# One ring of three PSUM slots, seven results turned into x by a transposing DMA, and new orders for the later stages of a sparse-attention + FFN kernel

## The chip, the core and the metric

The kernel runs on one core of one Trainium2 chip. A core has a matrix engine (TensorE, PE in the profile, with PEld for its weight loads), a vector engine (VectorE, DVE), a scalar engine (ScalarE, ACT), GpSimd (POOL) and a sync engine (SyncE, SP) that here only issues DMAs. Each engine works through its own list of instructions in order and waits on semaphores. The metric is the device time of one launch in microseconds (us), as the median over runs.

## The reference

```python
scores = 1/sqrt(64) * q @ k^T             # 4 batches, 8 heads, 768 tokens, head size 64
mask   = |block_i - block_j| <= 1, or block 0 / 23 on either side, or one of 3 sampled blocks   # 24 blocks of 32
attn   = softmax(where(mask, scores, -1e9))
x      = (attn @ v), heads side by side    # 3072 tokens x 512
out    = gelu(x @ w_in) @ w_out            # 512 -> 2048 -> 512, exact gelu, float32 out
```

Blocks 0 and 23 of each batch see all 24 blocks (the dense ones); each of the other 22 sees eight blocks: first, last, its three neighbours and three sampled ones.

## The kernel before

The work is cut into eight units, two per batch, of 384 tokens each. An even unit holds the blocks 1 to 11 and both dense blocks of its batch, an odd one the blocks 12 to 22. The attention of unit n+1 runs beside the second matrix product (FFN2) of unit n; between two such stages stands the first product (FFN1) of the unit whose attention has just ended, alone on PE. So the kernel alternates: attention n+1 with FFN2 n, then FFN1 n+1, and so on, and a last FFN2 alone.

In an attention stage a unit is cut into rounds (two sparse blocks of 32 queries, or one dense block for half of the heads) and groups (a, b, c: up to four sparse blocks; d: the dense ones). The order on every engine is written by hand: `attention` walks through a string of words, `PLANS[n]`. The number behind a letter is a round, the letter behind it a group.

- s: scores of a round on PE into a PSUM tile `sc` (line 358). m: row maxima on DVE (384, dense 387). e: exponentials on ACT (401, dense 405). t: 32x32 turnings on DVE (418, 423).
- w: values on PE into a PSUM tile `av` (445 dense, 484). d: division by the row sums on DVE (499 to 504), which writes `xh`.
- o: `xh` is turned by four PE transposes into a PSUM tile `tx` (516) and copied by ACT into `xT` (524, 529), the input of FFN1. O: the same in two copies.
- f: some of the 48 FFN2 products (583). S: store of finished FFN2 tiles, if there are any (ACT copy 567, then a DMA on SP). G: the gelu table is loaded on ACT (429).

An FFN1 step (540) puts two products of 384 columns into a PSUM tile `hp`; ACT makes the gelu of it (562; 560 for the last step). FFN1 needs the whole `xT`, since each product runs over all 384 columns.

PSUM has eight banks. Tiles `sc`, most `hp` and a few `av` take turns in two slots of two banks each (`psA`); most `av` and one or two `hp` have a slot of their own (`psV`); `psT` and `psO` (one bank each) hold the FFN2 tile and, in the other one, `tx`. A tile can be written only when the reader of the tile that had its slot before is done.

During an FFN1 stage DVE copies keys and values that the next unit will see into a buffer `gb` (`gather_fixed`, lines 296 and 309, and `gather`, 317). After FFN1 of units 1 and 3, POOL also issues twelve loads of later queries and keys (127); a small copy `mark` on POOL (173) holds them back until `xT` of the unit's second but last group (group b) has been written. POOL's own copies into `gb` wait behind these loads. SP turns the loaded queries and keys by transposing DMAs (137, 134).

Of the kernel before, what the change touches and what calls it, by code (L numbers as in the profile page):

```python
# [10 lines left out]
F32 = mybir.dt.float32  # L11
# [9 lines left out]
def kernel(  # L21
# [42 lines left out]
    psA = ctx.enter_context(tc.tile_pool(name="psA", bufs=2, space=PSUM))  # L64
    psV = ctx.enter_context(tc.tile_pool(name="psV", bufs=1, space=PSUM))
# [201 lines left out]
    def spaces():  # L267

        def banks():
            return [psT.tile([P, PI, PP], BF16, name="pt", tag="T"),  # L270
                    psO.tile([P, PI, PP], BF16, name="pt", tag="op")]
        views = [psA.tile([P, 2, 1024], BF16, name="pk", tag="A")[:, 0, 0:S].rearrange(
            "p (i c) -> p i c", i=PI) for _ in range(2)]
        yield from views + banks()
        two = psV.tile([P, 2, 1024], BF16, name="pq", tag="V")
        two = [two[:, i, 0:S].rearrange("p (i c) -> p i c", i=PI) for i in range(2)]
        yield from two[0:1] + banks() + two[1:2]
# [61 lines left out]
    closing = [unit for unit in units if unit.dense or unit.b == B - 1]  # L339
# [91 lines left out]
    def values(unit, grp, halves, ends_last=False):  # L431
        kv = kvs[unit.b % 2]
        if 0 in halves:

            pool, tag = (psA, "A") if unit in closing and grp == unit.ends[len(unit.rounds) - 1] else (psV, "V")
            st[grp, "av"] = pool.tile([P, 2, 512], F32, name="av", tag=tag)
# [57 lines left out]
    def divided(grp):  # L494
        av, n, m = st.pop((grp, "av"))
        rows = slice(0, 32 * n)
        a = av[rows, :, 0:VS * m // 2].rearrange("p h (g v) -> p h g v", v=VS)
        den = small.tile([P, 2, 4], F32, name="den")
        nc.vector.tensor_scalar_add(den[rows, :, 0:m].rearrange("p h (g x) -> p h g x", x=2),
                                    a[:, :, :, 2 * D:V2], 1e-9)  # L500
        rec = small.tile([P, 2, 4], F32, name="rec")
        nc.vector.reciprocal(rec[rows, :, 0:m], den[rows, :, 0:m])
        xh = small.tile([P, 2, 4 * D], BF16, name="xh")
        nc.vector.tensor_tensor(  # L504
            xh[rows, :, 0:m * D].rearrange("p h (g x d) -> p h g x d", x=2, d=D),
            a[:, :, :, 0:2 * D].rearrange("p h g (x d) -> p h g x d", d=D),
            rec[rows, :, 0:m].rearrange("p h (g x) -> p h g x", x=2)[:, :, :, :, None].to_broadcast([32 * n, 2, m // 2, 2, D]),
            op=ALU.mult)
        st[grp, "xh"] = xh, n, m

    def outputs(unit, grp, parts=1):
        xh, n, m = st.pop((grp, "xh"))
        T = turning_bank([P, 2, 2, P], "tx")
        for h in range(2):
            for G in range(m // 2):
                nc.tensor.transpose(T[:, G, h, 0:32 * n],  # L516
                                    xh[0:32 * n, h, P * G:P * G + P],
                                    identity[0:32 * n, 0:32 * n])
# [12 lines left out]

    opened, covered = {}, {}

    def ffn1_tile(n, m):
        pool, tag = (psV, "V") if m == (4 if n else 2) else (psA, "A")
        return pool.tile([P, 2, 512], F32, name="hp", tag=tag)
# [14 lines left out]
    def ffn1_step(n, m):  # L551
        T = P * len(units[n].quads)
        hp = opened.pop(m) if m in opened else ffn1_tile(n, m)
        last = psV.tile([P, 2, 512], F32, name="hp", tag="V") if m == KOUT - 2 else None
# [45 lines left out]
    def last_output(n):  # L600
# [5 lines left out]
                 psV.tile([P, 2, D_MODEL], F32, name="av", tag="V")[:, 0],  # L606
# [9 lines left out]
    def attention(unit, filler, plan, extra={}, ahead=None):  # L616
# [12 lines left out]
        for word in plan.split():  # L629
# [32 lines left out]
            elif what in "oO":  # L662
                outputs(unit, groups[arg], 1 + (what == "O"))
            todo.remove(word.lower())
# [79 lines left out]
    def next_keys(b):  # L744
# [108 lines left out]
```

## Time and profile before

| | |
|---|---|
| median of 3 runs | 274.27 us (274.2 to 274.39) |
| span of the profiled execution, first to last instruction | 271.9 us |
| time of the profiled execution beside its span | not given apart; the median of the runs is 2.4 us above the span |
| PE / ACT / DVE / POOL busy | 255.1 / 207.0 / 203.2 / 103.0 us |
| FFN1 stages (each, from 72.2 us on) | 10.4 us, PE busy throughout |
| attention stages of units 2 to 7 | 20.3, 18.0, 20.0, 17.9, 19.8, 17.0 us |

A stage is read in the table of windows: the share of an engine's busy time in it says which engine could bound it, and the chain of waits which one did. PE is busy 94% of the span, but a busy engine is not always on time: what counts is where PE's next instruction had to wait for another engine.

### The profile page before, as it was taken

The numbers are of one execution on the slowest core, as the hardware profiler recorded it, in microseconds if no ns is written. First come the engines' busy times: TensorE is split into PE (matmuls) and PEld (weight loads), VectorE is DVE, ScalarE is ACT, GpSimd is POOL, SyncE is SP. The second block draws the span as 40 slices with busy tenths as digits, with TensorE's granted clock in tenths as the row PEclk, the third lists the DMA queues.
The fourth block names the chain that finished last, engine by engine and source line by source line (L and its number), as shares of the span: only waits on it lengthen the run. The fifth ranks groups of instructions, "written<-read, shape, count | busy, mean of one in ns | idle before, by whom it ended". The sixth has DMA issues, their size and how long they took to land.

```text
span 271.9 us, 11545 instructions
## 1 busy us (share of the span) xinstructions
PE 255.1 (94%) x4944; PEld 144.8 (53%) x4944; DVE 203.2 (75%) x472; ACT 207.0 (76%) x379; POOL 103.0 (38%) x212
## 2 busy tenths in 40 slices
PE   0789699999999999999999999999999999999995
PEld 0634485455664665545554466455645655465544
DVE  7599758699896989589998987698939993882000
ACT  8789746977868886797868976988788966995611
POOL 7798960735964000950963002920040160000000
PEclk9999979999999999999999999999999999999999
DMA  6999399979999115951999108911101110111012
GB/s 98 185 185 144 66 140 201 206 129 146 95 172 129 41 43 122 122 65 50 104 164 123 60 28 159 112 43 45 40 0 41 46 41 0 41 41 43 0 40 78
DMA packets 75909, 24.40 MB, mean 90 GB/s; under 512 B 65489, under 2 KB 72914, under 8 KB 75858
## 3 DMA queue, kind: packets, MB, share of 16 engines
q0 software_dynamic: 57440, 13.64, 53.7%
q1 hardware_dynamic: 18418, 10.03, 15.5%
q8 instruction: 38, 0.62, 1.0%
q14 instruction: 13, 0.11, 0.1%
HBM read 27.26 MB, written 6.29 MB: 123 GB/s over the span
## 4 chain that ended last, share of the span: by engine, by line
PE 71%; DMA 9%; ACT 7%; POOL 6%; issue 4%; DVE 2%; POOLq 1%; ACTq 0%
PE hp L540 27%; PE op L583 21%; PE av L484 9%; DMA kn<-in_k_dram 6%; PE sc L358 4%; DMA kv<-in_v_dram 3%; ACT L429 2%; PE tx L516 2%; PE op L612 2%; PE av L445 2%; POOL g L317 2%; ACT pp L401 2%; PE pt L242 1%; POOL kv L149 1%; PE av L612 1%
## 5 line engine op out<-in xcount | busy, mean ns | idle before, releaser
L540 PE MATMUL hp<-xT,w_in_sb 128*128 128x384 bf16 (+2 forms) x536 | 85.1, 319 | 0.2 <-issue 0.2
L583 PE MATMUL op<-w_out_sb,g 128*128 128x512 bf16 x336 | 83.9, 380 | 0.4 <-issue 0.4
L401 ACT ACTIVATE pp<-sc,nm 128x256 bf16<-128x256 f32 x176 | 74.4, 546 | 7.5 <-DVE nm L384 7.5
L540 PEld LDWEIGHTS <-w_in_sb 128*128 128x128 bf16 x536 | 51.2, 98 | 33.3 <-issue 0.3
L562 ACT ACTIVATE g<-hp 128x768 bf16<-128x768 f32 x56 | 45.2, 809 | 25.4 <-PE hp L540 25.4
L384 DVE TENSOR_REDUCE nm<-sc 128x4 f32<-128x1024 f32 (+1 forms) x48 | 53.2, 1117 | 10.5 <-PE sc L358 10.2
L583 PEld LDWEIGHTS <-g 128*128 128x128 bf16 x336 | 28.6, 98 | 34.3 <-issue 7.2
L317 DVE COPY gb<-kv 128x392 bf16 x177 | 34.7, 274 | 0.0
L418 DVE STREAM_TRANSPOSE pT<-pp 128x512 f32<-128x512 f32 (+1 forms) x48 | 31.2, 657 | 4.3 <-ACT pp L401 3.8
L317 POOL COPY gb<-kv 128x392 bf16 x54 | 26.3, 537 | 16.1 <-PE av L484 15.7
L173 POOL COPY mark<-gb 1x1 bf16<-1x1 bf16 x6 | 1.1, 178 | 81.3 <-DVE gb L317 81.3
L484 PE MATMUL av<-kv,pT 64*32 64x130 bf16 (+1 forms) x1344 | 28.7, 228 | 1.0 <-DVE pT L418 0.9
L484 PEld LDWEIGHTS <-pT 64*32 64x32 bf16 (+1 forms) x2400 | 26.8, 94 | 5.1 <-DVE pT L418 2.6
L149 POOL DMA_DIRECT2D kv<-in_v_dram x32 | 22.9, 726 | 2.4 <-issue 2.3
L524 ACT COPY xT<-tx 128x512 bf16<-128x512 bf16 (+1 forms) x32 | 13.9, 459 | 11.6 <-PE tx L516 11.3
L358 PE MATMUL sc<-gb,qT 64*32 64x256 bf16 x704 | 18.4, 274 | 2.9 <-issue 1.5
L358 PEld LDWEIGHTS <-qT 64*32 64x32 bf16 x832 | 9.5, 89 | 21.2 <-issue 13.4
L429 ACT ACT_TABLE_LOAD x15 | 19.2, 1283 | 0.2
L387 DVE TENSOR_REDUCE nm<-sc 128x1 f32<-128x768 f32 x16 | 14.7, 947 | 5.9 <-PE sc L358 5.7
L504 DVE TENSOR_TENSOR xh<-av,rec 128x512 bf16<-128x512 f32 (+2 forms) x28 | 18.3, 652 | 1.0
L567 ACT COPY os<-op 128x512 f32<-128x512 f32 (+1 forms) x23 | 13.1, 570 | 6.0 <-PE op L612 4.3
L484 PE MATMUL av<-gb,pT 64*32 64x130 bf16 x924 | 17.2, 222 | 0.0
(80 smaller groups left out, 249.6 us busy)
## 6 DMA issues: line engine op xcount, KB each, us to landing
out_dram<-os SPq DMA_DIRECT2D x23, 256.0 KB, 2.4
kv<-in_v_dram POOLq DMA_DIRECT2D x32, 96.0 KB, 3.7
w_in_sb<-in_moe_w_in_dram POOLq DMA_DIRECT2D x4, 512.0 KB, 7.3
w_out_sb<-in_moe_w_out_dram POOLq DMA_DIRECT2D x2, 1024.0 KB, 13.4
kn<-in_k_dram POOLq DMA_DIRECT2D x4, 384.0 KB, 11.4
qn<-in_q_dram POOLq DMA_DIRECT2D x4, 384.0 KB, 12.8
qn<-in_q_dram POOLq DMA_DIRECT2D x12, 128.0 KB, 4.9
kn<-in_k_dram POOLq DMA_DIRECT2D x12, 128.0 KB, 6.0
```

Source lines behind the costliest of these rows:

```text
L149: nc.gpsimd.dma_start(out=kvs[b % 2][32 * hh:32 * hh + 32, 0:NB, c0:c0 + D], in_=v[b, h].rearrange("(n p) d -> p n d", p=BL))
L317: (engine or nc.vector).tensor_copy(to[:, None, :], src[:, bass.ds(at[j][r], 1), :])
L358: nc.tensor.matmul(o, lhsT=qT[rows, j // 4, pr, BL * (j % 4):BL * (j % 4) + BL], rhs=rhs(rows, pr), start=True, stop=True)
L384: nc.vector.tensor_reduce(out=nm[:, 0:2 * n].rearrange("p (g j) -> p g j", g=2), in_=A4[:, :, 0:n, :], op=ALU.max, axis=AX.X, negate=True)
L401: nc.scalar.activation(at[:, x // n, x % n], A[:, a:a + 256].rearrange("p (e c k) -> p e c k", e=2, k=BL), AF.Exp, bias=nm[:, x:x + 1])
L418: nc.vector.transpose(pt.rearrange("p g c x -> p (g c) x")[:, :, 64 * s:64 * (s + n)].bitcast(F32), pp[:, 0:512 * n].bitcast(F32).rearrang ...
L429: nc.scalar.activation(junk, zero[0:1, 0:1], func)
L484: nc.tensor.matmul(av[32 * s:32 * (s + w), h, VS * G:VS * G + V2], lhsT=pv[rows, G, c % 4, BL * s:BL * (s + w), c // 4], rhs=src[rows], st ...
L504: nc.vector.tensor_tensor(xh[rows, :, 0:m * D].rearrange("p h (g x d) -> p h g x d", x=2, d=D), a[:, :, :, 0:2 * D].rearrange("p h g (x d) ...
L540: nc.tensor.matmul(hp[:, i, c0:c1], lhsT=w_in_sb[:, ki, (m + i) * P:(m + i + 1) * P], rhs=xTs[n % 2][:, ki, c0:c1], start=(ki == 0), stop= ...
L562: nc.scalar.activation(g[:, m:m + 2, 0:T], hp[:, :, 0:T], AF.Gelu)
L583: nc.tensor.matmul(op, lhsT=g[:, m, t * P:(t + 1) * P], rhs=w_out_sb[:, m, :], start=(m == 0), stop=(m == KOUT - 1))
```

## The change

1. `psV` is gone. `psA` has three slots of two banks, and all tiles `sc`, `av` and `hp` take them in turn, in the order of the program.
2. A new word y: `xh` of a group of four blocks goes into `xT` by one transposing DMA on SP instead of four PE transposes and an ACT copy. `xh` is laid out anew, so that one DMA can read it. The plans hold y five times; three units share one of the plans, so seven transposes run: groups b and a of unit 1, b of units 2, 4 and 6, a and b of unit 7.
3. The plans of units 2 to 7 are new. Units 2, 4 and 6 have one plan, and so have 3 and 5. The plan of unit 1 differs in the two words y alone, that of unit 0 not at all.

```diff
-    psA = ctx.enter_context(tc.tile_pool(name="psA", bufs=2, space=PSUM))
-    psV = ctx.enter_context(tc.tile_pool(name="psV", bufs=1, space=PSUM))
+    psA = ctx.enter_context(tc.tile_pool(name="psA", bufs=3, space=PSUM))
...
-            pool, tag = (psA, "A") if unit in closing and grp == unit.ends[len(unit.rounds) - 1] else (psV, "V")
-            st[grp, "av"] = pool.tile([P, 2, 512], F32, name="av", tag=tag)
+            st[grp, "av"] = psA.tile([P, 2, 512], F32, name="av", tag="A")
...
-        xh = small.tile([P, 2, 4 * D], BF16, name="xh")
+        xh = small.tile([P, 2, 2, 2 * D], BF16, name="xh")
...
+    def turned_outputs(unit, grp):
+
+        xh, n, _ = st.pop((grp, "xh"))
+        xT, t0 = column[unit.b, grp[0][1][0]]
+        nc.sync.dma_start_transpose(out=xT[:, :, t0:t0 + 32 * n],
+                                    in_=xh[0:32 * n].rearrange("p g h c -> p (g h c)"))
+
...
     def ffn1_tile(n, m):
-        pool, tag = (psV, "V") if m == (4 if n else 2) else (psA, "A")
-        return pool.tile([P, 2, 512], F32, name="hp", tag=tag)
+        return psA.tile([P, 2, 512], F32, name="hp", tag="A")
...
+            elif what == "y":
+                turned_outputs(unit, groups[arg])
+                word = "o" + arg
...
-        3: ("s0 m0 s1 e0 m1 f13 e1 s2 t0 m2 e2 f5 t1 s3 m3 f3 wa S t2 s5 m5 e3 f8 da e5 f1 t3 s4 f2 m4 wb  "
-            "f5 e4 oa t5 db s6+7 S f1 ob t4 wc m7 e7 m6 f6 dc e6 Oc f1 t6 G t7"),
+        3: ("f1 s0 s1 s2 f3 m0 f2 e0 m1 f1 S f2 m2 f2 e1 f2 t0 f3 e2 f4 t1 s4 s5 f1 m4 e4 f4 m5 e5 f1 s3 t2 "
+            "m3 f9 t4 wa t5 wc e3 f1 da f1 oa f3 dc t3 f1 oc S s7 wb m7 db e7 s6 f1 m6 f3 Ob e6 t7 G t6"),
```

The plan of units 2, 4 and 6 ends now in `... t5 s7 wb f1 m7 e7 dd f2 oa f1 S f3 t6 f1 t7 G wc od f1 db yb f3 dc f1 Oc f1`.

The first place is the list of SP, from the turning of unit 3's queries (line 137 before, 136 now) to that of the next keys (134, 133): stage 2, before.

```order
L137 DMA_TRANSPOSE qT_89<-qn 128x24x128
L569 DMA out_dram<-os 128x512 x3
L134 DMA_TRANSPOSE ptd<-kn 128x24x128
```

The same place now; line 533 is the word y, line 572 a store.

```order
L136 DMA_TRANSPOSE qT_86<-qn 128x24x128
L572 DMA out_dram<-os 128x512 x2
L533 DMA_TRANSPOSE xT_91<-xh 128x4x128
L572 DMA out_dram<-os 128x512
L133 DMA_TRANSPOSE ptd<-kn 128x24x128
```

One transpose of 4 tiles of 128x128 stands ahead of the stage's last store; the larger ones have 24 such tiles.

The second place is the end of stage 3 on DVE, before: a turning of group c (418), the two dense maxima of the next unit (387), the division of group c (499 to 504), the two dense turnings (423), and then the copies for unit 4 (296 is the first).

```order
L418 STREAM_TRANSPOSE pT<-pp 128x8x64
L387 TENSOR_REDUCE nm<-sc 128x1 x2
L499 TENSOR_SCALAR den<-av 96x8
L502 RECIPROCAL rec<-den 96x8
L504 TENSOR_TENSOR xh<-av,rec 96x512
L423 STREAM_TRANSPOSE ptd<-pp 128x12x32 x2
L296 COPY gb<-kv_86 128x4x3x128 x2
```

The same place now (416 for 418, 385 for 387, 496 to 501 for 499 to 504, 421 for 423, 295 for 296).

```order
L416 STREAM_TRANSPOSE pT<-pp 128x8x64
L385 TENSOR_REDUCE nm<-sc 128x1
L496 TENSOR_SCALAR den<-av 128x8
L499 RECIPROCAL rec<-den 128x8
L501 TENSOR_TENSOR xh<-av,rec 128x2x2x128
L385 TENSOR_REDUCE nm<-sc 128x1
L421 STREAM_TRANSPOSE ptd<-pp 128x12x32 x2
L295 COPY gb<-kv_83 128x4x3x128 x2
```

The turning ahead is one of group b now. Group b (128 partitions) is divided last, not group c (96), and one dense maximum comes behind it.

The third place is the same end of stage 3 on ACT, before: an exponential of group c, the copies of `xT` (524) for a and b, the two dense exponentials (405), the copies for c, the gelu table (429).

```order
L401 ACTIVATE pp<-sc,nm 128x2x4x32 x4
L524 COPY xT_95<-tx 128x4x128 x2
L405 ACTIVATE pp<-sc,nm 128x12x2x32 x2
L524 COPY xT_95<-tx 128x2x96 x2
L429 ACT_TABLE_LOAD
```

And now, with an exponential of group b first (399 for 401, 521 for 524, 403 for 405, 427 for 429):

```order
L399 ACTIVATE pp<-sc,nm 128x2x4x32 x4
L521 COPY xT_92<-tx 128x4x128
L521 COPY xT_92<-tx 128x4x96
L403 ACTIVATE pp<-sc,nm 128x12x2x32
L521 COPY xT_92<-tx 128x2x128 x2
L403 ACTIVATE pp<-sc,nm 128x12x2x32
L427 ACT_TABLE_LOAD
```

The last copies of `xT` are those of group b now, and one dense exponential stands behind them, ahead of the table.

More of the change, by code (lines that the diff above doesn't have):

```diff
@@ L274, in spaces @@
         yield from views + banks()
-        two = psV.tile([P, 2, 1024], BF16, name="pq", tag="V")
+        two = psA.tile([P, 2, 1024], BF16, name="pq", tag="A")
         two = [two[:, i, 0:S].rearrange("p (i c) -> p i c", i=PI) for i in range(2)]
@@ L338 @@
              for quads, dense in (((1, 2, 0), True), ((3, 4, 5), False))]
-    closing = [unit for unit in units if unit.dense or unit.b == B - 1]
     groups_of = {rnd: grp for unit in units for grp in unit.ends.values() for rnd in grp}
@@ L502, in divided @@
         nc.vector.reciprocal(rec[rows, :, 0:m], den[rows, :, 0:m])
-        xh = small.tile([P, 2, 4 * D], BF16, name="xh")
+        xh = small.tile([P, 2, 2, 2 * D], BF16, name="xh")
         nc.vector.tensor_tensor(
-            xh[rows, :, 0:m * D].rearrange("p h (g x d) -> p h g x d", x=2, d=D),
+            xh[rows, 0:m // 2].rearrange("p g h (x d) -> p h g x d", d=D),
             a[:, :, :, 0:2 * D].rearrange("p h g (x d) -> p h g x d", d=D),
@@ L516, in outputs @@
                 nc.tensor.transpose(T[:, G, h, 0:32 * n],
-                                    xh[0:32 * n, h, P * G:P * G + P],
+                                    xh[0:32 * n, G, h],
                                     identity[0:32 * n, 0:32 * n])
@@ L553, in ffn1_step @@
         hp = opened.pop(m) if m in opened else ffn1_tile(n, m)
-        last = psV.tile([P, 2, 512], F32, name="hp", tag="V") if m == KOUT - 2 else None
+        last = psA.tile([P, 2, 512], F32, name="hp", tag="A") if m == KOUT - 2 else None
         for i in range(2):
@@ L605, in last_output @@
         banks = [psO.tile([P, D_MODEL], F32, name="op", tag="op"),
-                 psV.tile([P, 2, D_MODEL], F32, name="av", tag="V")[:, 0],
+                 psA.tile([P, 2, D_MODEL], F32, name="av", tag="A")[:, 0],
                  psA.tile([P, 2, D_MODEL], F32, name="hp", tag="A")[:, 0],
```

27 rows, old and new, of the table PLANS are left out of this document.

## The prediction

> **What bounds the kernel now.** I read the page's busy times and its chain first, then the table of windows by stage, then the timeline of each engine at the joints between stages.
>
> ```profile
> PE 255.1 (94%) x4944; PEld 144.8 (53%) x4944; DVE 203.2 (75%) x472; ACT 207.0 (76%) x379; POOL 103.0 (38%) x212
> PE 71%; DMA 9%; ACT 7%; POOL 6%; issue 4%; DVE 2%; POOLq 1%; ACTq 0%
> ...
> core 0: us, PE busy (x) PEld busy (x) DVE busy (x) ACT busy (x) POOL busy (x), PEclk, DMA share, GB/s
> 82.60:102.90 20.30, 20.15 (x564) 11.11 (x565) 17.54 (x31) 17.43 (x37) 2.33 (x6) 1.00 0.46 68
> 113.30:131.30 18.00, 17.82 (x466) 9.07 (x462) 15.71 (x25) 15.88 (x34) 8.53 (x17) 1.00 0.55 62
> 131.30:141.70 10.40, 10.40 (x72) 6.14 (x70) 10.33 (x32) 7.62 (x11) 8.73 (x10) 1.00 2.08 154
> 141.70:161.70 20.00, 19.77 (x563) 10.64 (x564) 17.93 (x33) 17.39 (x37) 2.91 (x7) 1.00 0.51 79
> 190.10:200.50 10.40, 10.40 (x72) 6.14 (x70) 7.41 (x33) 7.62 (x11) 2.44 (x7) 1.00 0.07 26
> 200.50:220.30 19.80, 19.69 (x564) 10.72 (x565) 17.69 (x30) 17.47 (x37) 4.06 (x9) 1.00 0.09 30
> 230.70:247.70 17.00, 16.93 (x450) 9.09 (x450) 13.11 (x21) 14.91 (x33) 0.00 (x0) 1.00 0.09 34
> ```
>
> PE bounds it. In the attention stages of units 2, 4 and 6 (20.3, 20.0, 19.8 us) PE is 99% busy at the full clock, and DVE and ACT carry 17 to 18 us each, so a later start of DVE has about two microseconds to hide in and no more. FFN1 stages are PE alone, 10.4 us; a third slot gives them nothing, because PE never waits there. One of them stands out: ahead of unit 4 (131.3 to 141.7) DVE is busy for 10.33 of 10.40 us, against 7.41 ahead of unit 6, with the same copies.
>
> **The steps of a stage.** For the new orders I need durations. They come from unit 7's stage, which starts at 230.61, from unit 3's and from unit 2's:
>
> ```profile
> 230.61 0.63 PE L358 MATMUL sc<-gb,qT 64*32 64x256 bf16 x32
> 231.18 3.19 PE L583 MATMUL op<-w_out_sb,g 128*128 128x512 bf16 x14
> 234.34 0.41 PE L358 MATMUL sc<-gb,qT 64*32 64x256 bf16 x16
> 234.68 1.69 PE L583 MATMUL op<-w_out_sb,g 128*128 128x512 bf16 x7
> ...
> 247.53 1.79 PE L540 MATMUL hp<-xT,w_in_sb 128*128 128x384 bf16 x10
> ...
> 119.56 0.70 PE L484 MATMUL av<-kv,pT 64*128 64x130 bf16 x32
> 120.75 0.30 PE L358 MATMUL sc<-gb,qT 64*32 64x256 bf16 x8
> ...
> 90.15 1.73 PE L445 MATMUL av<-kv,ptd 64*64 64x130 bf16 x96
> 91.81 0.39 PE L583 MATMUL op<-w_out_sb,g 128*128 128x512 bf16 x1
> ...
> 232.62 3.19 ACT L401 ACTIVATE pp<-sc,nm 128x256 bf16<-128x256 f32 x8
> 235.68 0.55 ACT L567 COPY os<-op 128x512 f32<-128x512 f32 x1
> ...
> 234.95 1.18 DVE L384 TENSOR_REDUCE nm<-sc 128x4 f32<-128x1024 f32 x1
> 236.06 0.69 DVE L418 STREAM_TRANSPOSE pT<-pp 128x512 f32<-128x512 f32 x1
> 236.78 1.23 DVE L384 TENSOR_REDUCE nm<-sc 128x4 f32<-128x1024 f32 x1
> ...
> 241.08 0.15 DVE L499 TENSOR_SCALAR den<-av 128x8 f32<-128x8 f32 x1
> 242.11 0.70 DVE L418 STREAM_TRANSPOSE pT<-pp 128x512 f32<-128x512 f32 x1
> ```
>
> From start to start: an FFN2 product 0.226 (14 in 3.16), a sparse score round 0.34, values of a full sparse group 1.19, dense values 1.66, an exponential round 1.53 (two in 3.06), a sparse maximum 1.11, a turning 0.65 to 0.7, a division 1.03. The first exponential comes 2.0 us into a stage (232.62 - 230.61), behind gelu and table load; no order changes that. I count a stage from the start of PE's first instruction in it to the start of FFN1's first: 16.9 for unit 7 (230.61 to 247.53), where the table has 17.0 for it; so I take 0.1 off the table's other stages too: 20.2, 17.9, 19.9, 17.8 and 19.7 for units 2 to 6.
>
> **Units 2, 4 and 6 (one plan).** Count from the moment when PE leaves FFN1. DVE starts at 0.86 and runs without a break: two dense maxima (1.8, by the row of 142.25 below), three sparse ones (3.3), two dense turnings (about 1.1, a little under the sparse ones) and two sparse ones (1.3), at 8.4. Only then are the values of group a ready. PE has put 26 products (5.9) and six score rounds (2.2) behind it by 8.1, so it waits 0.3. From 8.45: values a 1.19, scores 0.34, six products 1.36, dense values 1.66, half a score round 0.24, values b 1.19, three products 0.7, an output 0.23, five products 1.13, values c 1.05, dense output 0.11, five products 1.13, output c 0.2, three products 0.7. That is 19.7. The three-slot ring costs nothing here: each slot's reader (an exponential or a division) ends ahead of the tile that follows in it.
>
> The last part is the transpose. DVE reaches the division of b at 15.8, behind the last turning, which needs the last exponential; `xh` is ready at 16.9, and FFN1's first product needs all of `xT`. SP's queue is free then (its store goes out at about 13.5). What 4 tiles take, no trace of before shows. The nearest rows are the transposes of 24 tiles and the plain stores of 256 KB:
>
> ```profile
> L134 SPq DMA_TRANSPOSE ptd<-kn x2: 3942/4162/4382, 104.2 to 163.0; - x2
> DMA to landing us min/median/max: 5.9/6.5/7.1
> ...
> DMA to landing us min/median/max: 1.7/2.3/5.0
> ```
>
> So it lands 1.7 to 7.1 us after its issue. It is a small transfer, nearer to the store; a sixth of the 4.2 us by which 24 tiles exceed the store's 1.7 gives 2.4, by the medians 3.0; I take 2.9 with the semaphore. It lands at 19.8 to 20.0 where PE is ready at 19.7: 0.3 of waiting, 0 to 3.2 by the bounds. Behind it on SP stand the stage's last store and the next keys' transpose; both wait for work of FFN1 or later, so the 0.7 us of its issue cost them nothing. The new layout of `xh` leaves DVE the same 512 elements to write: 0. Sum for the plan: 20.0. Against 20.2, 19.9 and 19.7 that is -0.2, +0.1 and +0.3, before what follows.
>
> What is saved by y on PE is read around an output of before:
>
> ```profile
> 100.79 0.40 PE L516 MATMUL tx<-identity,xh 128*128 128x128 bf16 x4
> 101.02 1.03 PE L583 MATMUL op<-w_out_sb,g 128*128 128x512 bf16 x4
> ```
>
> 0.23 us of PE each, and an ACT copy that was hidden. In unit 1, where only this changes, that is -0.45 for two; there the transposes start at 66 and have until FFN1 at 71.6.
>
> **Units 3 and 5 (one plan).** PE's sum in order: a product 0.3, three score rounds 0.9, 19 products 4.2, two rounds 0.6, six products 1.4, a round 0.3, nine products 2.0, values a and c 2.2, two products 0.45, output 0.25, four products 0.9, output 0.2, dense scores 0.4, values b 1.2, dense scores 0.35, four products 0.9, output b 0.25, three products 0.7: 17.5. I find no wait above 0.1 in it, because DVE and ACT run ahead; before it was 17.9 and 17.8. -0.4 and -0.3.
>
> **Unit 7.** The same walk meets three waits: values b wait for a turning at 9.6 (0.15), values c for the last one at 13.6 (0.5), output c for its division (0.35). 17.3 against 16.9 before, although the outputs of a and b cost PE nothing now: +0.4. The transposes are issued by 14 and hidden.
>
> **The joint from unit 3 to unit 4.** This is where I see the largest term.
>
> ```profile
> 128.53 0.18 POOL L173 COPY mark<-xT 1x1 bf16<-1x1 bf16 x1 [9.12 <-ACT xT L524]
> 129.06 5.64 POOL L127 DMA_DIRECT2D qn<-in_q_dram  x6 [0.35 <-issue]
> 134.68 5.34 POOL L127 DMA_DIRECT2D kn<-in_k_dram  x6
> ...
> 131.35 2.27 DVE L296 COPY gb<-kv 128x1536 bf16<-128x1536 bf16 x3
> 134.97 6.99 DVE L317 COPY gb<-kv 128x392 bf16 x27
> 142.25 1.82 DVE L387 TENSOR_REDUCE nm<-sc 128x1 f32<-128x768 f32 x2 [0.28 <-PE sc L358]
> ...
> 134.97:140.02 5.05, 5.05 (x17) 0.00 (x0) 1.00 2.20 181
> 140.02:141.96 1.94, 1.94 (x12) 0.00 (x0) 1.00 2.41 158
> ```
>
> DVE's 32 copies for unit 4 begin 0.2 us after FFN1 does and end 0.28 us before unit 4's first maximum is asked for: no slack. While POOL issues its loads (to 140.02), 16 copies took 5.05 us, 0.316 each; after that 11 took 1.94, 0.176 each. The new plan 3 divides b last, puts an exponential behind b's copies and two turnings behind that. By the walk output b is at 16.6, `xT` of b at 17.5, that exponential ends at 18.6 and the turnings at 19.15, where FFN1 began at 17.5: DVE starts its copies 1.65 us into FFN1 instead of 0.2. And POOL's loads wait for `xT` of b, which came 2.6 us ahead of FFN1 before and comes with it now, so they cover nearly the whole of DVE's copies. 1.65 + 3.6 for the first five, then 6.3 us of slowed copies (20 of 27), then 7 at 0.176: 12.8 us, against FFN1's 10.4. Unit 4's first maximum starts at 2.45 instead of 0.86, 1.6 us late. In the walk above DVE is the engine that PE waits for from there on, so nothing absorbs it: +1.6 for unit 4. Least would be 0.7, if the copies weren't slowed any more than before; at most 2.2.
>
> The Trainium skill, SBUF — State Buffer, section Who interferes with whom, says that a DVE copy in a two-port mode and GpSimd lock each other out of a shared port pair for a whole instruction. By this rule the copies are slowed for as long as POOL issues, wherever that is moved, and the term stays 1.6; the two rates above agree with it.
>
> At unit 2's joint POOL's loads move too (they wait for a DMA now): copies end at about 82.6, the first maximum is due at 82.9, so 0. Ahead of unit 6 there are no such loads.
>
> **The sum.** -0.45 (unit 1) - 0.2 (2) - 0.4 (3) + 0.1 + 1.6 (4) - 0.3 (5) + 0.3 (6) + 0.4 (7) = +1.05. The last FFN1 and FFN2 stay. The span of 271.9 becomes 272.9; the runs' median (274.27) is 2.4 above the span, so 275.3.
>
> **Rivals.** One: DVE isn't late in unit 4, because it catches up or the copies are not slowed. The seven saved outputs and the new orders then stand alone: 275.3 - 1.6 = 273.7; with the transposes landing in time too (0.3 in three units) 272.8, faster. For it: DVE has 2 us of idle time in that stage; against it: this idle time lies behind the point where PE first waits for DVE. It decides if the copies end less than 0.7 us after FFN1 does.
>
> Two: the transposes land late. At 3.9 us instead of 2.9, the end of units 2, 4 and 6 is 1 us later each: 278.3. At the 5.9 of the 24-tile rows it would be 3 us each, 284.3; against that, their issue alone is 4 us, which four tiles can't need.
>
> The Trainium skill, VectorE: DVE Perf Modes, section The three transpose paths, advises TensorE for a 128x128 transpose and gives 1309 ns for one by DMA. By that, as an estimate, four would take 5.2 us, 2.3 more than my 2.9 in three units, and the time would be near 282; I give that 0.02 of this rival's chance. The trace disagrees: 24 tiles issue in 3.9 to 4.4 us, 0.17 each.
>
> Three: nothing comes of it: PE's order is full before and after, and each wait only moves. 274.3.
>
> **Chances.** The forecast (274.5 to 276.5, likeliest 275.3) 0.5, rival one (272.8 to 273.7) 0.2, two 0.17, three 0.13. About 0.2% (0.55 us) is what a measurement of this kernel can tell. Slower than 274.8: 0.43 of the forecast's 0.5 and all of rival two, 0.6. Faster than 273.7: nearly all of rival one, 0.18. The rest, 0.22, is three and the edges of the others. The range takes in most of rival one and the nearer half of two, and leaves out the lowest and the farthest: 273.2 to 277.6.
>
> **What would show it.** The profile after should have PE outputs (516) in 76 instructions instead of 104; FFN1 stages of 10.4; DVE's first maximum of unit 4 some 2.4 us after FFN1's end; stages of units 2 to 7 of 20.0, 17.5, 21.6, 17.5, 20.0 and 17.3 us by the same count; a DMA wait of PE of under a microsecond ahead of FFN1 of units 2, 4 and 6. The forecast is wrong if unit 4 takes no longer than unit 6, or if these DMA waits are above 1 us.

## The result, and the profile after

| | before | after |
|---|---|---|
| median | 274.33 us (4 runs) | 278.78 us (4 runs, 277.79 to 279.68) |
| ratio | | 1.0147, 95% interval 1.0109 to 1.0184 |
| span of the profiled execution | 271.9 us | 276.2 us |
| FFN1 of unit 1 to the end, in that execution | 199.84 us | 204.73 us |

The changed kernel is 4.4 us slower, where 1.05 was predicted. By the same count as in the prediction (from the end of one FFN1, 10.49 us, to the start of the next), with the waits above 0.2 us that the next section explains in a column of their own. The last two columns are of both kernels with fewer instructions on PE (e9 and e10 below):

| stage of unit | before | predicted | after | of it waits for instructions | before, PE's instructions cut | after, PE's instructions cut |
|---|---|---|---|---|---|---|
| 2 | 20.2 | 20.0 | 20.9 | 0.6 | 19.9 | 19.2 |
| 3 | 17.9 | 17.5 | 17.9 | 0 | 17.8 | 17.9 |
| 4 | 19.9 | 21.6 | 22.6 | 1.0 | 19.7 | 20.8 |
| 5 | 17.8 | 17.5 | 17.9 | 0 | 17.9 | 17.8 |
| 6 | 19.7 | 20.0 | 20.5 | 0.8 | 19.5 | 19.8 |
| 7 | 16.9 | 17.3 | 17.3 | 0 | 16.8 | 17.1 |

The page of the profile after: busy times, and the chain that ended last.

```profile
PE 249.6 (90%) x4880; PEld 143.1 (52%) x4916; DVE 203.1 (74%) x472; ACT 202.3 (73%) x372; POOL 102.0 (37%) x212
...
PE 43%; DVE 18%; DMA 13%; POOL 13%; issue 10%; ACT 1%; POOLq 1%; DVEq 1%; ACTq 0%
```

"issue" is time in which an engine waited for nothing that the profile shows. It was 4% of the chain before and is 10% now. The chain also runs over other engines now, so this share is a hint and not the length of PE's waits. The table of windows, by the stages of the table shown of before:

```profile
core 0: us, PE busy (x) PEld busy (x) DVE busy (x) ACT busy (x) POOL busy (x), PEclk, DMA share, GB/s
82.00:102.90 20.90, 19.07 (x554) 10.56 (x557) 18.31 (x34) 17.21 (x37) 3.38 (x8) 1.00 0.76 97
113.40:131.30 17.90, 17.09 (x461) 9.37 (x465) 14.89 (x24) 14.28 (x33) 5.68 (x13) 1.00 0.49 58
131.30:141.80 10.50, 10.50 (x65) 6.21 (x64) 9.55 (x23) 8.83 (x13) 10.10 (x12) 1.00 1.52 118
141.80:164.40 22.60, 19.11 (x555) 10.32 (x559) 19.73 (x43) 17.38 (x38) 3.94 (x9) 1.00 0.74 94
203.30:223.80 20.50, 18.80 (x555) 10.20 (x559) 17.01 (x31) 16.81 (x37) 6.31 (x14) 1.00 0.14 35
234.30:251.60 17.30, 16.15 (x437) 8.29 (x442) 13.08 (x21) 13.87 (x31) 0.00 (x0) 1.00 0.17 49
```

PE was busy for 99% of the dense stages and is for 91%, 85% and 92% of units 2, 4 and 6. (36 of 4,916 product records are missing in this trace, which exaggerates it.) PE's timeline shows three kinds of waits:

```profile
93.07 1.53 PE L442 MATMUL av<-kv,ptd 64*64 64x130 bf16 x93
95.18 0.25 PE L442 MATMUL av<-kv,ptd 64*64 64x130 bf16 x3 [0.58 <-issue]
...
102.92 1.31 PE L543 MATMUL hp<-xT,w_in_sb 128*128 128x384 bf16 x7 [0.41 <-DMA xT<-xh]
...
146.33 0.41 PE L356 MATMUL sc<-gb,qT 64*32 64x256 bf16 x16 [1.18 <-ACT pp L403]
...
158.78 1.03 PE L586 MATMUL op<-w_out_sb,g 128*128 128x512 bf16 x4
160.56 0.38 PE L586 MATMUL op<-w_out_sb,g 128*128 128x512 bf16 x1 [0.75 <-issue]
...
214.41 1.48 PE L442 MATMUL av<-kv,ptd 64*64 64x130 bf16 x89
216.10 0.31 PE L442 MATMUL av<-kv,ptd 64*64 64x130 bf16 x7 [0.21 <-issue]
```

One is the transposing DMA (0.41). One is the late DVE of unit 4 (1.18 us ahead of the third score round). The third was not predicted: PE stops in the middle of the dense values, behind 93 or 89 of 96 products that write one tile, where nothing of another engine can be missing. The same occurs in a run of FFN2 products at 160.56 and, not shown, at 219.83 (0.60).

The joint of units 3 and 4, DVE and POOL:

```profile
133.04 2.52 DVE L295 COPY gb<-kv 128x1536 bf16<-128x1536 bf16 x3
...
136.91 7.36 DVE L316 COPY gb<-kv 128x392 bf16 x27
144.19 1.81 DVE L385 TENSOR_REDUCE nm<-sc 128x1 f32<-128x768 f32 x2
...
131.88 5.63 POOL L126 DMA_DIRECT2D qn<-in_q_dram  x6 [0.35 <-issue]
137.49 5.34 POOL L126 DMA_DIRECT2D kn<-in_k_dram  x6
```

FFN1 of unit 3 began at 131.26 and ended at 141.75. The copies start 1.78 us into it, POOL's loads run beside nearly all of them, and the first maximum of unit 4 comes 2.44 us behind FFN1's end: foretold were 1.65 and 2.45.

The transposing DMAs, from the view of line 533 (issue in ns, min/median/max):

```profile
L533 SPq DMA_TRANSPOSE xT<-xh x7: 1195/1197/2266, 66.5 to 248.8; - x7
...
DMA to landing us min/median/max: 2.4/3.4/4.3
```

### The profile page after: what moved, and what is told of

Its sections match the earlier page's. It is cut to its first block, busy times and chain, and to the rows that moved or that the text cites. A ratio compares the mean times of both kernels' runs of the same rounds, so it can differ in the third digit from the quotient of the medians.

```text
span 276.2 us, 11489 instructions
## 1 busy us (share of the span) xinstructions
PE 249.6 (90%) x4880; PEld 143.1 (52%) x4916; DVE 203.1 (74%) x472; ACT 202.3 (73%) x372; POOL 102.0 (37%) x212
## 3 DMA queue, kind: packets, MB, share of 16 engines
q1 hardware_dynamic: 22226, 10.95, 16.8%
## 4 chain that ended last, share of the span: by engine, by line
PE 43%; DVE 18%; DMA 13%; POOL 13%; issue 10%; ACT 1%; POOLq 1%; DVEq 1%; ACTq 0%
PE op L586 12%; PE hp L543 11%; PE av L481 8%; DVE gb L316 6%; DMA kn<-in_k_dram 6%; DVE nm L382 4%; POOL kv L148 4%; PE sc L356 3%; POOL gb L316 3%; DMA kv<-in_v_dram 3%; DMA qn<-in_q_dram 3%; DVE nm L385 2%; PE op L615 2%; PE av L442 2%; POOL g L316 2%
## 5 line engine op out<-in xcount | busy, mean ns | idle before, releaser
L586 PE MATMUL op<-w_out_sb,g 128*128 128x512 bf16 x301 | 75.5, 380 | 5.3 <-issue 5.0
L399 ACT ACTIVATE pp<-sc,nm 128x256 bf16<-128x256 f32 x176 | 73.4, 541 | 6.7 <-DVE den L496 4.6
L316 DVE COPY gb<-kv 128x392 bf16 x177 | 36.9, 287 | 0.0
L416 DVE STREAM_TRANSPOSE pT<-pp 128x512 f32<-128x512 f32 (+1 forms) x48 | 30.3, 648 | 2.1 <-ACT pp L399 2.1
L316 POOL COPY gb<-kv 128x392 bf16 x54 | 25.0, 515 | 12.3 <-PE av L481 12.0
L403 ACT ACTIVATE pp<-sc,nm 128x768 bf16<-128x768 f32 x16 | 17.0, 1108 | 5.1 <-DVE nm L385 5.1
L521 ACT COPY xT<-tx 128x192 bf16<-128x192 bf16 (+3 forms) x25 | 9.6, 416 | 15.1 <-PE tx L513 15.1
L427 ACT ACT_TABLE_LOAD x15 | 19.2, 1283 | 0.3
```

What stands on the lines that cost most here:

```text
L316: (engine or nc.vector).tensor_copy(to[:, None, :], src[:, bass.ds(at[j][r], 1), :])
L399: nc.scalar.activation(at[:, x // n, x % n], A[:, a:a + 256].rearrange("p (e c k) -> p e c k", e=2, k=BL), AF.Exp, bias=nm[:, x:x + 1])
L416: nc.vector.transpose(pt.rearrange("p g c x -> p (g c) x")[:, :, 64 * s:64 * (s + n)].bitcast(F32), pp[:, 0:512 * n].bitcast(F32).rearrang ...
L427: nc.scalar.activation(junk, zero[0:1, 0:1], func)
L586: nc.tensor.matmul(op, lhsT=g[:, m, t * P:(t + 1) * P], rhs=w_out_sb[:, m, :], start=(m == 0), stop=(m == KOUT - 1))
```

## The experiments

Theory F is the one for the third kind of wait: PE runs through its own instructions faster than they are brought in. The page after has a queue for them:

```profile
q8 instruction: 38, 0.62, 1.0%
```

That is 38 transfers of 16 KB. PE's list in the built program (weight loads, products and semaphore instructions) has 9,878 entries, 260 for each transfer. The Trainium skill, Runtime: NRT & Kernel Launch, section Terms, says that an engine's instruction memory is refilled in blocks of 16 KiB. The trace agrees with it.

**Shifting the blocks (e1).** In the changed kernel:

```diff
     nc.vector.memset(zero, 0.0)
+    first = psO.tile([P, D_MODEL], F32, name="op", tag="op")
+    for _ in range(64):
+        nc.tensor.matmul(first[0:1, 0:1], lhsT=zero, rhs=zero, start=True, stop=True)
```

> Edit: 64 one-element products on PE (128 PE instructions with their weight loads) ahead of all other work, while PE has nothing to do (in the changed kernel its first product is at 6.29 us); results are the same. Theory F (PE runs out of fetched instructions): in the changed kernel PE's unexplained waits (94.60 for 0.58 us, 155.98 for 0.29, 159.80 for 0.75, 215.89 for 0.21, 219.23 for 0.60, 247.71 for 0.31) all begin at a count of PE instructions that is 206 to 234 above a multiple of 256; with 128 instructions more they must leave these places (dense values of units 2, 4, 6; the FFN2 products ahead of values c in units 4 and 6; values c of unit 7) and stand 128 PE instructions earlier or later, again at that remainder, each 0.8 to 1 us behind the end of a 16 KB instruction transfer. The time may move by up to 1.5 us either way. Rival H (a hidden wait for a slot, DVE or ACT): the waits stay at the same instructions with the same lengths, and the time is within 0.3 us of 278.8.

Measured: 292.33 us, 1.063 of the kernel before (1.058 to 1.068). 64 products that ended at 2.7 us, in PE's idle time, made the kernel 13.5 us slower. Theory F had allowed 1.5 us either way, so it missed the size; rival H (no change) is out. The waits of PE's values, and one of them in the timeline:

```profile
PE av L484 <- issue: 13.0, 8, 2.4
```

```profile
98.29 0.26 PE L484 MATMUL av<-kv,pT 64*32 64x130 bf16 x5
100.40 0.35 PE L484 MATMUL av<-kv,pT 64*32 64x130 bf16 x19 [1.85 <-issue]
```

The waits left their places, and the waits for DVE, ACT and POOL (1.18 us at the third score round of unit 4) stayed at theirs. All 4,916 weight loads of the changed kernel are recorded (4,980 here), so each wait can be placed in PE's list. These are all waits above 0.2 us from 26 us on to the last FFN1 that have no releaser, but for one of 0.25 us ahead of the same score round of unit 1 in each (64.92 and 67.39): the number of the weight load behind each, and its remainder by 256.

```
changed kernel   962 (194)  1475 (195)  3523 (195)  5827 (195)  6083 (195)  8131 (195)  8387 (195)
e1               1475  2243  3779  4803  5059  6083  7107  7363  8387     (195 each)
```

So the place is settled: all these waits stand at a remainder of 194 or 195 (206 to 234 was expected), where a block begins. The trace also has the start and the end of each 16 KB transfer of q8, and they settle the cause. Where PE has 13 blocks behind it at a wait, 13 transfers are done, where it has 22 behind it, 22, and so on, so each wait can be set beside the transfer of the block that begins there. The changed kernel's seven waits again, in us:

```
end of the block's transfer     29.97  39.89  93.82  155.02  159.00  214.76  218.42
PE's first instruction of it    31.23  41.25  95.18  156.28  160.56  216.10  219.83
```

In all 75 waits of this kind above 0.25 us, in the twelve kernels with the full number of instructions, PE goes on 1.2 to 1.6 us behind the end of the transfer of just that block.

How the size comes about is seen where two waits follow each other. From the end of one to the end of the next there passed 4.28 us (156.28 to 160.56), 3.73 (216.10 to 219.83) and, in e1, 3.46 (161.81, a wait of 0.18, to 165.27). In no profile here does a transfer begin less than 3.2 us behind the one before it. The new plan of units 2, 4 and 6 puts values a, a score round, the dense values, another round and values b with few products between them: some 680 weight loads and products in 6.0 us by the prediction's durations, 256 in 2.3. Before, the longest such run was values b and c, some 390. The difference is one of degree, though: with the products between its runs, the densest 6.0 us of before hold 640, 636 and 610 weight loads and products in units 2, 4 and 6, and no wait above 0.2 us stands there.

**Fewer instructions (e9 before, e10 after, e11 after with e1's products).** The same edit in each, in the changed kernel's lines; the sparse values likewise run for G = 0 alone over 262 columns. The values are not the attention's then, and only the time is read:

```diff
-            for c in range(NB // 2 * halves[0], NB // 2 * (halves[-1] + 1)):
+            for c in range(NB // 2 * halves[0], NB // 2 * (halves[-1] + 1), 2):
...
-                        nc.tensor.matmul(av[64 * G:64 * G + 64, h, 0:V2],
+                        nc.tensor.matmul(av[64 * G:64 * G + 64, h, 0:VS + V2],
...
-                                         rhs=kv[rows, c, c0:c0 + V2],
+                                         rhs=kv[rows, c, KC:KC + VS + V2],
```

> Edit, in the kernel before: the values are made by half as many products, each twice as wide (262 columns for 130; dense: every other key block, sparse: the weights of the first half of the heads alone). PE streams the same number of columns with 7106 instructions instead of 9890; everything else, the waits for and of the values among it, stands as it was. The values are not the attention's any more, and only the time is read. Theory F: no two blocks of 256 PE instructions are run through within 3.8 us any more, no wait for instructions is left; before loses its own (about 2.4 us in its profile): 271.5 to 272.8 us. Rival H: 274.4, or more if wide products stream slower.

> The same edit (half as many values' products, twice as wide; values not the attention's) in the changed kernel: 7050 PE instructions instead of 9834. Theory F: its waits for instructions go too (4.7 us in its profile, more in some runs); what stays above the kernel before with the same edit is the rest of the loss, 1.3 to 2.3 us, nearly all of it in unit 4: 273.2 to 274.8 us. Rival H (the waits are part of the new orders): the distance between the two stays 4 us or more.

> The changed kernel with the same halved values, and with the 64 one-element products of PE ahead that cost the changed kernel 13.5 us (values not the attention's). Theory F: with fewer instructions it doesn't matter any more where the blocks of 256 lie; within 0.5 us of the halved kernel without the 64 products. Rival: whatever else these products did, they cost 5 us or more again.

Measured: 273.72 (0.9964, 0.9936 to 0.9991), 275.25 (1.0023, 0.9991 to 1.0054) and 272.61 us (0.9939, 0.9915 to 0.9962). e9 and e10 lie 0.9 and 0.45 us above what theory F expected of each, but the distance between the two kernels fell from 4.4 to 1.5 us, as F has it and H has not. No wait of the third kind is left in units 2 to 7 of e10, whose page has

```profile
q8 instruction: 27, 0.44, 0.7%
```

From FFN1 of unit 1 to the end, e10 takes 200.07 us and e9 198.93: 1.14 apart, where the full kernels are 4.89 apart. The edit takes 3.75 us more from the changed kernel than from the one before; 2.43 of them are the waits themselves in the profile after (the column above), the rest must be what they delay, which no run separates.

The 64 products cost nothing now, as F has it, but e11 is 2.6 us faster than e10, and neither theory expected that. In both, PE leaves FFN1 of unit 0 early and waits for the FFN2 weights. This is e10:

```profile
51.35 1.24 PE L585 MATMUL op<-w_out_sb,g 128*128 128x512 bf16 x5 [3.10 <-DMA w_out_sb<-in_moe_w_out_dram]
```

In e11 this wait is 1.44 us. The windows show the granted clock (the third number from the end), first e10, then e11:

```profile
40.00:56.00 16.00, 12.59 (x118) 6.08 (x117) 10.07 (x32) 9.73 (x18) 5.40 (x18) 0.90 1.23 205
```

```profile
40.00:56.00 16.00, 13.86 (x142) 7.17 (x143) 11.29 (x34) 11.33 (x20) 5.38 (x18) 1.00 1.23 204
```

So the clock was lower around the longer wait. The executions bear this out: e10's five at a mean granted clock of 0.999 or more took 273.3 to 274.2 us and its four at 0.988 or less 275.8 to 277.3, and e11's nine at 0.997 or more took 272.2 to 272.9. By this some 1.2 of the 2.6 us stay at the full clock, and the rest goes with the clock. What shortened the wait itself, no run shows.

**The joint of units 3 and 4 (e2, e3, e12).** e2 gives unit 3 its old plan. e3 changes one number, and e12 does the same on top of e10:

```diff
-                    xT, t0 = column[b, unit.groups[-2][0]]
+                    xT, t0 = column[b, unit.groups[0 if n == 3 else -2][0]]
```

> Edit: unit 3's plan alone is that of before. Theory L (unit 4 is late because DVE and POOL's loads start late behind the new end of unit 3): DVE's first copy for unit 4 starts within 0.4 us of FFN1's start instead of 1.8 after it, the first maximum of unit 4 within 1 us of FFN1's end instead of 2.4, and unit 4's stage gets 1.7 to 2.3 us shorter (22.3 to about 20.3, near unit 6's 20.25); the total 276.5 to 277.1. Rival P (the plan of unit 4 itself, or the ring, makes it long): unit 4's stage keeps 22.0 us or more, total within 0.4 of 278.8.

> Edit: at the joint of units 3 and 4 POOL's small copy waits for x of group a instead of group b; nothing else. It parts the two halves of the +1.6 of the prediction. Theory L1 (contention): POOL issues its twelve loads 3 to 4 us earlier, about 127.5 to 138, so that fewer of DVE's 27 copies run beside them (some 8 instead of 20); DVE ends 1.4 to 1.8 us sooner though it starts as late as in the changed kernel; unit 4 gets 1.2 to 1.8 us shorter, total 277.0 to 277.6. Theory L2 (the late start of DVE is all): the copies end at the same time, unit 4 keeps its 22.3, total 278.8.

> The changed kernel with the same halved values (not the attention's), and POOL's loads at the joint of units 3 and 4 held by x of group a instead of group b. With no waits for instructions about, the total should tell what this joint is worth. Theory L1 (POOL's loads beside DVE's copies make DVE late): 1.2 to 1.8 us below the halved changed kernel, all of it in unit 4. Theory L2 (the late start of DVE alone): no change.

Measured: 278.36 us (1.0121, 1.0078 to 1.0165), 278.65 (1.0116, 1.0065 to 1.0168) and 273.77 (0.9975, 0.9949 to 1.0). The totals of e2 and e3 hardly moved and missed what theories L and L1 expected. The stages answer as these theories say, though: in e2 DVE starts its copies 0.21 us into FFN1, the 27 copies take 6.99 us as before, and unit 4's stage goes from 22.6 to 21.3 us (L had 20.3); in e3 it goes to 20.6. Other waits for instructions grew in their place (in e3's profile, which is of its longest execution, 2.45 us among the FFN1 products of unit 0, 0.61 in the changed kernel's). With those out of the way, e12 is 1.5 us below e10, all of it in unit 4 (19.2 us for 20.8). Its joint, DVE, POOL and PE:

```profile
132.90 2.05 DVE L295 COPY gb<-kv 128x1536 bf16<-128x1536 bf16 x3
...
136.30 5.88 DVE L316 COPY gb<-kv 128x392 bf16 x27
142.46 1.82 DVE L385 TENSOR_REDUCE nm<-sc 128x1 f32<-128x768 f32 x2 [0.28 <-PE sc L356]
...
127.77 5.27 POOL L126 DMA_DIRECT2D qn<-in_q_dram  x6 [0.35 <-issue]
132.97 5.71 POOL L126 DMA_DIRECT2D kn<-in_k_dram  x6
...
144.94 0.41 PE L356 MATMUL sc<-gb,qT 64*32 64x256 bf16 x16
```

DVE starts 1.78 us into FFN1, as late as in the changed kernel, and still is in time, because the 27 copies take 5.88 us instead of 7.36: POOL issues beside them for 2.4 us only, not for 5.9. So the loss needs the contention with POOL. The late start is not free either: by these rows, copies as slow as those of before (6.99 us) would have made DVE 0.83 us late (6.99 - 5.88 - 0.28).

The Trainium skill, SBUF — State Buffer, section Who interferes with whom, says that a DVE copy in a two-port mode and GpSimd lock each other out of a shared port pair. The runs agree that these copies are slower while POOL issues; whether they run in such a mode, no run shows.

**The transposing DMA (e4, e15).** In both, y becomes o again in units 2, 4 and 6 (e15 on top of e10):

```diff
-            "f1 db yb f3 dc f1 Oc f1"),
+            "f1 db ob f3 dc f1 Oc f1"),
```

> Edit: in units 2, 4 and 6 group b is turned by PE and copied by ACT again (word o for y); the transposing DMAs of units 1 and 7 stay. Theory T (as in the prediction: the DMA lands late by some 0.4 us and saves 0.23 us of PE): the wait of 0.41 us ahead of FFN1 of unit 2 goes, and PE has 0.23 us more work in each of three stages; total -0.6 to +0.3 us against 278.8. Rival T2 (the DMA is the main cost of these stages, 0.9 us each): total -1.5 to -2.7 us.

> Edit: the changed kernel with halved values' products (values not the attention's) and group b of units 2, 4 and 6 turned by PE again. With all instructions the same edit cost 3.4 us. Theory F: that was the place of the blocks; with the instructions cut the edit costs what PE has more to do less what it no longer waits for, 3 times 0.23 less 0 to 0.4: -0.3 to +0.7 us against the halved changed kernel (275.25). Rival T2 (outputs by DMA are worth a microsecond each): +2 to +3 us.

Measured: 282.12 us (1.026, 1.0216 to 1.0304), outside both expectations, and 275.25 (1.0017, 0.999 to 1.0044), the same as e10. In e4 eight more instructions in each of three stages moved the blocks; in its profile, which is of its longest execution, unit 6 alone has waits of 1.00 and 2.17 us where blocks begin. With few instructions the total is the same whether PE or the DMA turns group b. That is a balance: by the profiles of e15 and e10, units 2 and 4 are 0.6 us longer with PE, 3 and 5 0.55 shorter and 7 1.0 longer, and no run says why.

**The ring (e5, e13).** The kernel before with the ring alone, and the same with halved values:

```diff
-    psA = ctx.enter_context(tc.tile_pool(name="psA", bufs=2, space=PSUM))
-    psV = ctx.enter_context(tc.tile_pool(name="psV", bufs=1, space=PSUM))
+    psA = ctx.enter_context(tc.tile_pool(name="psA", bufs=3, space=PSUM))
```

> Edit: the kernel before with the one ring of three PSUM slots and nothing else (plans and outputs of before). PE has the same number of instructions as before. Theory R0 (as in the prediction: the ring by itself costs and saves nothing): 273.9 to 274.8 us. Rival R1 (the ring makes PE or DVE wait for slots, and is a part of the changed kernel's loss): 275.3 or more, with waits of PE for DVE or ACT that before does not have.

> Edit: the kernel before with the ring of three slots, and with the values made by half as many products, twice as wide (values not the attention's). Theory R0 with F (the ring costs nothing; the 1.8 us that it showed with all instructions are waits for instructions): within 0.6 us of the kernel before with halved products (273.7), and its stages of units 2 to 7 within 0.2 us of that kernel's. Rival R1 (the ring itself costs): 1.2 to 2 us above it.

Measured: 276.19 us (1.0054, 1.0027 to 1.008) and 273.19 (0.9937, 0.9905 to 0.997; e9 has 273.72). e13's stages of units 2 to 7 are within 0.2 us of e9's. In e5 unit 5 is 1.9 us longer, through a wait in the middle of a score round:

```profile
179.89 0.30 PE L357 MATMUL sc<-gb,qT 64*32 64x256 bf16 x7
181.50 0.28 PE L357 MATMUL sc<-gb,qT 64*32 64x256 bf16 x1 [1.32 <-issue]
```

It stands at number 6850 of PE's list, 194 above a multiple of 256. The ring has ten more semaphore instructions in the list (I had expected the same number), which is enough to move it there. By itself it costs nothing.

**Better places for the blocks (e6, e7, e8).** I walked the recorded weight loads with blocks of 256 and a least distance of 3.5 to 3.9 us, and chose kernels by it. e6 is the kernel before with six products ahead, e7 the changed kernel with 122, e8 the kernel before with seven and

```diff
-... f4 od f2  m5 s6 wa e5 f3 t4 m6 da s7 f1 e6 m7 t5 t6 e7 t7 f4 oa wb wc G f1 db dc ob f4 Oc
+... f4 od f2 m5 s6 wa e5 f3 t4 m6 da ya s7 f1 e6 m7 t5 t6 e7 t7 f4 wb wc G f1 db dc ob f4 Oc
```

in units 2, 4, 6 and 7 alike (here unit 2), and the plan of unit 1 of the changed kernel.

> Edit: the kernel before with six one-element products of PE (12 instructions) ahead of all other work. Theory F (a block of 256 PE instructions can't be had sooner than some 3.5 to 3.9 us behind the block before it, so that a wait falls due where PE runs through 256 instructions faster than that): walking before's own PE instructions with its blocks laid 12 instructions earlier, the sum of these waits is 1.5 us less (0.8 of it in unit 0, between 26 and 36 us): 272.5 to 273.2 us. Rival H (the products do nothing): 274.3 within 0.3.

> Edit: the changed kernel with 122 one-element products (244 instructions, so that the blocks of 256 lie 12 instructions later than in the changed kernel) ahead of all other work, in PE's idle first 6.2 us. The same edit with 64 products cost 13.5 us. Theory F: by the same walk the waits in units 2 to 7 fall by 0.8 to 2.0 us: 276.8 to 278.0 us. A theory by which the extra products themselves cost time: above 292 us.

> Edit: the kernel before (two slots and one, its own plans) with the word y where its time is plentiful: groups b and a of unit 1 as in the changed kernel, and group a of units 2, 4, 6 and 7, asked for right behind the division; seven one-element products (14 instructions) ahead of all other work. Theory F with the prediction's 0.23 us for each output that PE no longer turns: six outputs save 1.4 us, and by the walk the blocks of PE's instructions lie so that the waits for them fall by another 1.6 us: 270.9 to 272.0 us, below both kernels. Rival T2 (the transposing DMA itself costs what the changed kernel lost): 275 us or more. Rival N (an output on PE is hidden anyway): 274.3.

Measured: 276.35 us (1.0076, 1.0047 to 1.0105), 279.02 (1.0175, 1.0132 to 1.0218) and 274.99 (1.0026, 1.0 to 1.0052). All three missed. e8 lies at the edge of T2 (275 or more), but no product of its profile waits for a transposing DMA, while waits for instructions of 2.21 and 2.06 us stand in unit 0. Only one part held: from FFN1 of unit 1 on e7 takes 203.47 us, 1.26 below the changed kernel. The walk finds the places, but with one fixed distance it can't tell a microsecond: the waits in unit 0 came out longer, where the DMA engines are busiest (e6: 1.23 and 1.10 us, from 30.15 and 39.92 on). And e8's four early outputs of group a shortened none of their stages.

**Both causes in a kernel that computes everything (e16), and the part that gains (e14).** e16 is the changed kernel with e3's line and 122 products ahead; e14 the kernel before with e3's line and the changed plan of unit 1 (`yb` for `ob`, `ya` for `oa`), the word y and the layout of `xh` with it.

> Edit: the changed kernel, computing everything, with POOL's loads held by x of group a and 122 one-element products of PE ahead (the blocks 12 instructions later). Both theories add: unit 4 is 1.6 us shorter, units 2 to 7 have 1.3 us fewer waits for instructions, so from FFN1 of unit 1 to the end some 201.8 us instead of 204.7; total 275.5 to 277.3, by how unit 0's waits fall. If they don't add, 278 or more.

> Edit: the kernel before with the word y for groups b and a of unit 1 alone, and POOL's loads at the joint of units 3 and 4 held by x of group a; nothing else. By the prediction's own step for unit 1 (two outputs of 0.23 us) and nothing from the joint (DVE ends its copies in time there before, too): 273.9. Theory F warns that 16 fewer instructions move the blocks for all later units: by the walk -0.4 to +0.4 us. Together 273.5 to 274.3. Rival: the moved blocks cost more than the two outputs gave, 275 or more.

Measured: 277.21 us (1.0088, 1.0056 to 1.012) and 273.72 (0.9957, 0.9929 to 0.9986). e16 lies at the upper end of what both theories together expect, 1.6 us below the changed kernel. From FFN1 of unit 1 on it takes 203.1 us, not 201.8: FFN1 now waits for the transposing DMA in units 2, 4 and 6, where other waits had hidden it.

```profile
103.70 1.47 PE L546 MATMUL hp<-xT,w_in_sb 128*128 128x384 bf16 x8 [0.79 <-DMA xT<-xh]
...
163.40 1.31 PE L546 MATMUL hp<-xT,w_in_sb 128*128 128x384 bf16 x7 [0.73 <-DMA xT<-xh]
...
222.41 1.80 PE L546 MATMUL hp<-xT,w_in_sb 128*128 128x384 bf16 x10 [0.71 <-DMA xT<-xh]
```

e14 is faster than both kernels, by 0.4% of the one before. Its two edits are not parted, and its blocks lie elsewhere too, so what the gain is due to stays open.

## Why the prediction was wrong

- **The sum.** Slower was right, the size was not. The step that failed is the walk through units 2, 4 and 6 (values a, scores, dense values and values b in a row, each at its duration of before, "from 8.45"). It had no term for how fast PE's instructions arrive. In its place the profile after shows 2.43 us of waits for blocks in these three stages, and with fewer instructions the changed kernel gains 3.75 us more than the one before. Durations of before hold only while the blocks come in time. With this limit out of the way in both kernels, the difference is 1.5 us (e10 and e9). That this is near the 1.05 of the sum is in part luck: up to FFN1 of unit 1 the two are 0.56 apart where the sum had -0.45, and the stages of units 2 to 7 differ by -0.8, +0.1, +1.1, -0.1, +0.3 and +0.3 where it had -0.2, -0.4, +1.7, -0.3, +0.3 and +0.4.
- **The joint of units 3 and 4** (+1.6) was right in place, mechanism and size: 1.5 us by e12. Its lower bound of 0.7, for copies slowed no more than before, is not tested: in e12 they are slowed less (5.88 us for 6.99), and by its rows the bound would be 0.8.
- **Unit 1** (-0.45): the profile after has -0.54 at FFN1 of unit 1, and e14, which rests on it, measured 0.4 to 1.9 us less than before by its interval. Neither isolates the two outputs: waits for instructions in units 0 and 1 differ as well.
- **The ring at nothing:** right (e13).
- **The transposing DMA:** landing 3.4 us for 2.9, issue 1.2 us for 0.7. A wait of 0.41 us was seen in unit 2 (0.3 predicted), and of 0.7 to 0.8 in e16. Mis-sized by half a microsecond, and hidden in units 4 and 6 by the waits for instructions.
- **Units 3 and 5** at 17.5, "no wait above 0.1": wrong. They took 17.9; in unit 5 PE waited 0.39 us for POOL's copies ahead of a score round that the new plan asks for earlier. In unit 3 no wait above 0.2 us shows; in e7, the same plan with the blocks elsewhere, it took 17.5.
- **Unit 7:** 17.3 predicted and measured. Of its three waits one shows above 0.2 us (values c behind a turning, 0.31 for 0.5), so the match of the total is in part luck.
- **The rivals.** Rival two gave nearly the measured time (278.3) by another cause, late transposes; they were half a microsecond late, not one. The 1309 ns that the Trainium skill gives for a 128x128 tile by DMA (VectorE: DVE Perf Modes, section The three transpose paths) would, as an estimate, have put four at 5.2 us. They landed after 3.4.

One wait is as long as its block's transfer is late. At the same place in unit 0 it was 0.17, 0.61, 1.62 and 2.45 us in the profiles of before, after, e2 and e3; the transfer ended at 39.65, 39.89, 40.55 and 41.50 us, and PE went on 1.3 to 1.4 us later each time. Open is what delays a transfer: these four began 3.9 to 5.2 us behind the first instruction of the block before, those at the waits of units 2 to 7 of the changed kernel 0.8 to 1.4.

## What to carry to other kernels

A stage made of many tiny matrix products can be limited by the arrival of PE's instructions, and the profile names no releaser for it: look for "issue" waits in the middle of a run of equal products, count the instructions between them, and look for the end of a transfer of the instruction queue just ahead of each. When they lie a multiple of 256 apart, thin out the burst. Where this limit is near, any edit that adds or drops a few PE instructions shifts it for all that follows, so undo edits one at a time only together with a kernel that has fewer instructions. And a copy beside POOL's DMA issues is priced by their overlap, so ask when the loads are issued before asking when the copies start.

## What the runs showed of the hardware

In the twelve kernels with the full number of PE instructions (before, after, e1 to e8, e14, e16) there are 80 waits of PE above 0.25 us between 20 us and the last FFN1 for which the profile names no releaser. 75 stand at 194 or 195 above a multiple of 256 in PE's list; the other five are one wait of 0.25 us ahead of the same score round of unit 1, in after and e1 to e4. At each of the 75, the transfer of the block that begins there had ended 1.2 to 1.6 us earlier. In the six kernels with fewer instructions none stands at such a place. The 16 KB transfers began at least 3.2 us behind one another in all 18 profiles. 64 one-element products took 1.7 us of idle time and cost 13.5 us further on, and cost nothing with 28% fewer instructions. The 27 copies of DVE took 7.36 us with POOL issuing DMAs beside them for 5.9 us, and 5.88 with it issuing for 2.4. The granted clock was 0.90 over 16 us around a PE wait of 3.1 us, and 1.00 around one of 1.4.
